# Attention and two MLPs on one core: the second MLP's weight units worked in place by a table of steps, and the first MLP's second product moved a step back

## The chip, the cores and the metric

The kernel runs on one core of a Trainium2 chip. Its time is device microseconds (us) of that core; the median of three runs of the kernel before is 884.52 us (882.35 to 887.07). The engines are named as in the profile: PE is TensorE (PEld its weight loads), DVE is VectorE, ACT is ScalarE, POOL is GpSimd, SP is SyncE, which here issues nearly all DMAs. PSUM is used as eight `banks` of 512 float32 columns.

## The reference

Attention within chunks of 64 tokens (4 x 8 heads, 576 tokens, head size 64), then two MLPs without biases over all 2304 tokens, width 512, hidden width 2048:

```python
scores = scale * np.matmul(q_c, k_c.transpose(0, 1, 2, 4, 3))
scores = scores - np.max(scores, axis=-1, keepdims=True)
attn = np.exp(scores)
attn = attn / (np.sum(attn, axis=-1, keepdims=True) + 1e-09)
out = np.matmul(attn, v_c)
...
h = x @ w_in            # first MLP
g = h - np.tanh(h)
return (g @ w_out).astype(np.float32)
...
h = x @ w_in            # second MLP
sp = np.where(h > 20.0, h, np.log1p(np.exp(np.minimum(h, 20.0))))
g = h * np.tanh(sp)
return (g @ w_out).astype(np.float32)
```

The weights arrive as float64.

## The kernel before

**Precision.** Each factor of a large product is split into a high part (a cast to float32r on ACT) and a low part (the float32 value less the high part), and a product is three matmuls (`THREE`). So every tensor that enters the large products costs a cast and a subtraction. A float64 weight is first turned into float32 in a "unit" of 128 x 1024 values: `turned` on ACT (the high word's exponent), `low` on DVE (the low word's three top bits by a shift), `joined` on DVE (both words into one).

**First MLP.** The 2304 tokens go in blocks of 512, 256, 512, 512, 512 (`BLOCKS`), the hidden width in 16 units f. A step s is one block and one f, 80 in all: `gemm1(s)` is 12 matmuls into one of two hidden banks, then h - tanh(h) by `gap_act` (ACT: z = Square, t = Tanh), `gap_mid` (DVE: g = z times h, t = h - t), `gap_poly` (ACT: m, z) and, one step later, `gap_end` (DVE: a scalar_tensor_tensor and a copy_predicated). `hi_part` casts g on ACT and `lo_part` makes its low part, on DVE for the first 32 steps and on POOL from there. `gemm2` of a step, 12 matmuls into banks 0 to 3, stands two steps behind its `gemm1` (`lag`). After a block's last step `evacuate` copies the four banks out on ACT into two or three single buffers (`e`, `et`, `ev`) and stores them to DRAM. The even weights stay in SBUF; from block 2 on the odd ones come back through a ring of three slots (`w_again`, 21 loads of 1 MB).

**Beside it.** Block 0 also turns the first MLP's weights. The 18 attention groups of 128 tokens (scores, max and exp, norm, transpose, values) run one block ahead, one per three steps. From step 35 on (`first_job`) the second MLP's 16 units run as jobs, a new one every 2.4 steps: load, `j_turned`, `j_low`, `j_float` into another buffer `jf`, `j_sums` (four slots made from sums and differences, for a seven-product scheme in the place of eight), and for the units of w_out `j_split`: cast on ACT, low parts on POOL. The results go to DRAM (`win`, `wout`).

**Second MLP.** Three passes of 768 tokens. In a pass the first phase (`group1`, four groups of 84 matmuls of 384 columns) makes g = mish, the second (`phase2`, 56 slots of 6 matmuls) multiplies by w_out, reading g through `g_split` (cast on ACT, low part on DVE, 384 columns each, three slots ahead). `x_split` and `wf_lo` part 1 make the low parts of x and of three of seven weight slots on POOL. At the end of `group1`'s last group three sums over g (`add`, `sub`, `sub`) come before phase 2's next splits on DVE.

**What sets the order.** Each engine runs its instructions in the order in which the code issues them; there is no scheduler. In a step that order is given by the lists `inner`, `cast`, `tail`, `job` (filled ahead, by step) and by the loop's body. SP's DMAs stand in one queue in the same order.

Of the kernel before, what the change touches and what calls it, by code (L numbers as in the profile page):

```python
# [13 lines left out]
I64 = mybir.dt.int64  # L14
AF = mybir.ActivationFunctionType
# [27 lines left out]
AHEAD = 4  # L43
# [3 lines left out]
def attn_moe_moe(ctx, tc, qkv, w1, w2, out):  # L47
# [12 lines left out]
    xp = es.enter_context(tc.tile_pool(name="x", bufs=2))  # L60
# [89 lines left out]
    streamed = [(b, f) for b in range(2, NB) for f in range(1, NF, 2)][RING:]  # L150
    ring = [(2, f) for f in range(1, 2 * RING, 2)] + streamed

    def w_again():

        while streamed:
            k = ring.index(streamed[0])
            b, f = ring[k - RING]
            if done <= b * NF + f:
                return
            W.pop(f)  # L160
            f = streamed.pop(0)[1]
            W.pop(f, None)
            W[f] = rp.tile([P, 2, 2 * DM], F32R, tag=f"r{k % RING}", name=f"w{f}", bufs=1)
            nc.sync.dma_start(out=W[f][:].bitcast(F32).rearrange("p c n -> p (c n)"), in_=w1s[f])


    JR, JF, SA, SB = {}, {}, {}, {}

    def j_load(n):
        JR[n] = pools["j"].tile([P, 2 * DM], I64, tag="raw", name="jraw", bufs=2)  # L170
        nc.sync.dma_start(out=JR[n], in_=w2[n])

    def j_turned(n):
        turned(JR[n])

    def j_low(n):
        low(JR[n])

    def j_float(n):
        t = JF[n] = pools["j"].tile([P, 8, 2 * P], F32, tag="jf", name="jf", bufs=2)  # L180
        joined(JR.pop(n), t[:, 1:5].rearrange("p q n -> p (q n)"))

    def j_sums(n):

        t = JF[n]
        sub(t[:, 5:7], t[:, 3:4].to_broadcast([P, 2, 2 * P]), t[:, 2:5:2])
        sub(t[:, 7], t[:, 4], t[:, 5])
        sub(t[:, 0], t[:, 1], t[:, 7])
        if n < NJ:
            JF.pop(n)  # L190
            nc.sync.dma_start(out=win[n][:, :4], in_=t[:, 4:])
            nc.sync.dma_start(out=win[n][:, 4:], in_=t[:, :3])

    def j_split(n, part):
        t = JF[n] if part == 0 else JF.pop(n)
        m, src = (4, t[:, 4:]) if part == 0 else (3, t[:, :3])
        o = (SA, SB)[part][n] = pools["j"].tile([P, 2, m, 2 * P], F32R, tag=f"s{part}", name="js", bufs=1)
        nc.scalar.copy(o[:, 0], src)
        sub(o[:, 1], src, o[:, 0].bitcast(F32), nc.gpsimd)

    def j_store(n, part):
        h, jj = divmod(n - NJ, 4)
        o = (SA, SB)[part].pop(n)
        m = (slice(0, 4), slice(4, 7))[part]
        for c in range(2):
            nc.sync.dma_start(out=wout[h][:, m, c, jj], in_=o[:, c].bitcast(F32))


    QKV, E, ET, MX, RD, BK = {}, {}, {}, {}, {}, {}
# [78 lines left out]
    def a_part(i, part):  # L288
        b = block_of[i]
        o = (i - first[b]) * P  # L290
        if (0, b) not in XL:
            XL[0, b] = xp.tile([P, 2, KD, TMAX], F32R, tag="x", name="x")
# [8 lines left out]
    steps = [(b, f) for b in range(NB) for f in range(NF)]  # L301
# [33 lines left out]
    def evacuate(b):  # L335

        t, o = BLOCKS[b], first[b] * P
        XL.pop((0, b), None)
        for m in range(KD):
            if b + 1 < NB:  # L340
                tag = ("e", "et", "ev")[m % (3 if "j" in pools else 2)]
                y = pools["j" if tag == "ev" else "a"].tile([P, TMAX], F32, tag=tag, name="ev", bufs=1)
            else:
                y = out_tile()[:].rearrange("p m n -> p (m n)")
            y = y[:, :t]
# [9 lines left out]
    def temp(s, tag, dt=F32):  # L355
        return ep.tile([P, TMAX], dt, tag=tag, name=tag)[:, :BLOCKS[steps[s][0]]]
# [11 lines left out]
    def gap_act(s):  # L368
# [16 lines left out]
    def hi_part(s):  # L385
        if max(lag(s), lag(s - 1)) > LAG and s % 2:
# [4 lines left out]
        nc.scalar.copy(o[:, 0, :BLOCKS[steps[s][0]]], GF[s])  # L391

# [11 lines left out]
    for f in range(NF - 2):  # L404
        w_load(f)
# [18 lines left out]
    def run(*todo):  # L424
# [11 lines left out]
        (a_load, lead), (a_load, lead + 1), (w_load, NF - 2), (w_load, NF - 1),  # L436
# [4 lines left out]
    inner, tail, head, mid, post = {}, {}, {}, {}, {}  # L441
# [4 lines left out]
    for b in range(1, NB):  # L446
        for q in range(BLOCKS[b] // P):
# [4 lines left out]
            at(tail, s, (a_first, i))  # L452
# [434 lines left out]
```

## Time and profile before

| | us |
|---|---|
| median of three runs | 884.52 |
| the profiled execution | 882.82 |
| its span on the core | 881.0 |
| PE busy | 816.8 (93%) |
| DVE busy | 673.2 (76%) |
| ACT busy | 501.9 (57%) |
| POOL busy | 192.6 (22%) |

The busy times are unions of instructions, so a matmul that is stretched counts as busy. The chain of work that ended last spends 47% of the span on PE and 33% on DVE. Step 0's `gemm1` starts at 24.9 us, block 2 (the first step with 512 columns after block 1) at 182, block 4 at 390; the last `gemm2` of the first MLP ends at 509.5 and the last matmul at 876.5. In the second MLP the three passes begin at 500, 635 and 758 and their second phases at 569, 693 and 816.

### The profile page before, as it was taken

What the parts mean: (1) busy time and instruction counts of PE and PEld (TensorE: products, weight loads), DVE (VectorE), ACT (ScalarE), POOL (GpSimd) and SP (SyncE); (2) the same over time, 40 slices, a digit from 0 to 9 for tenths busy, and PEclk for the clock granted to TensorE, in tenths of its full rate; (3) what the DMA queues carried; (4) which work ended last, traced back from release to release, by engine and by line L of the source; (5) the groups of instructions that cost most, each with busy time, mean ns of one, the idle gap of its engine ahead of it and who ended that gap; (6) DMA issues with size and microseconds to landing.
All of it is one profiled execution on the core that took longest, in us unless ns stands there. A gap on an engine that the chain in (4) does not pass through costs nothing.

```text
span 881.0 us, 13693 instructions
## 1 busy us (share of the span) xinstructions
PE 816.8 (93%) x5244; PEld 723.5 (82%) x5244; DVE 673.2 (76%) x952; ACT 501.9 (57%) x851; POOL 192.6 (22%) x128
## 2 busy tenths in 40 slices
PE   7899898999899989898997879989999999999997
PEld 6677688987677777676775679988999899999897
DVE  6999867866989888888964548778578787587663
ACT  4878865665566656566654544545545456445543
POOL 0001100011332332333335322123022042122000
PEclk9999999999999999999999999999999999999999
DMA  9964716636578787759582054487632787443783
GB/s 378 420 230 108 173 31 228 216 96 242 205 260 328 254 288 271 249 185 338 206 280 84 25 197 119 171 283 262 247 102 88 279 283 294 140 129 124 257 274 123
DMA packets 57777, 186.48 MB, mean 212 GB/s; under 512 B 4592, under 2 KB 32752, under 8 KB 44528
## 3 DMA queue, kind: packets, MB, share of 16 engines
q1 hardware_dynamic: 56272, 180.37, 58.2%
q0 software_dynamic: 1440, 5.24, 3.2%
q8 instruction: 41, 0.67, 0.3%
q14 instruction: 24, 0.20, 0.1%
HBM read 140.51 MB, written 39.85 MB: 205 GB/s over the span
## 4 chain that ended last, share of the span: by engine, by line
PE 47%; DVE 33%; ACT 6%; DMA 6%; issue 5%; POOL 2%; SPq 1%; ACTq 0%; DVEq 0%; POOLq 0%
PE banks L577 19%; PE banks L666 16%; PE banks L328 6%; PE banks L319 5%; DVE g L364 4%; DVE jf L81 4%; DVE jf L112 3%; DVE g L365 3%; DVE g L377 2%; DVE t L81 2%; DVE s L81 2%; DMA w<-wf 2%; DVE wf L112 1%; POOL xo L81 1%; DMA x<-ev 1%
## 5 line engine op out<-in xcount | busy, mean ns | idle before, releaser
L328 PE MATMUL banks<-go,w 128*128 128x512 f32 (+1 forms) x960 | 224.9, 382 | 15.2 <-POOL go L81 6.6
L319 PE MATMUL banks<-x,w 128*128 128x512 f32 (+1 forms) x960 | 216.4, 374 | 7.5 <-DMA w<-wf 2.7
L328 PEld LDWEIGHTS banks<-go,w 128*128 128x128 f32 x960 | 168.7, 192 | 55.6 <-POOL go L81 10.1
L319 PEld LDWEIGHTS banks<-x,w 128*128 128x128 f32 x960 | 168.3, 189 | 43.6 <-DVE w L81 3.9
L666 PE MATMUL banks<-s,w 128*128 128x384 f32 x1008 | 180.0, 339 | 11.4 <-DVE s L81 11.4
L666 PEld LDWEIGHTS banks<-s,w 128*128 128x128 f32 x1008 | 176.0, 190 | 15.0 <-DVE s L81 15.0
L577 PE MATMUL banks<-xo,w 128*128 128x384 f32 x1008 | 176.1, 334 | 4.7 <-ACT o L346 2.2
L577 PEld LDWEIGHTS banks<-xo,w 128*128 128x128 f32 x1008 | 174.9, 188 | 5.9 <-ACT o L346 2.6
L81 DVE TENSOR_TENSOR s<-g,s 128x384 fp32r<-128x384 f32 x168 | 96.6, 616 | 41.3 <-ACT s L654 41.0
L81 POOL TENSOR_TENSOR go<-g,go 128x512 fp32r<-128x512 f32 x48 | 61.9, 1290 | 264.4 <-ACT go L391 243.0
L654 ACT CAST s<-g 128x384 fp32r<-128x384 f32 x168 | 79.9, 511 | 47.6 <-PE banks L666 44.3
L391 ACT CAST go<-g 128x512 fp32r<-128x512 f32 (+1 forms) x80 | 46.2, 578 | 90.2 <-DVE g L365 90.1
L81 POOL TENSOR_TENSOR w<-wf,w 128x768 fp32r<-128x768 f32 x24 | 44.3, 1846 | 155.1 <-ACT w L550 149.2
L550 ACT CAST w<-wf 128x1024 fp32r<-128x1024 f32 (+1 forms) x48 | 44.8, 936 | 47.4 <-DMA wf<-win 31.5
L84 DVE TENSOR_TENSOR o<-o,banks 128x768 f32<-128x768 f32 x39 | 37.1, 951 | 40.5 <-ACT o L597 15.5
L377 DVE TENSOR_TENSOR g<-z,banks 128x512 f32<-128x512 f32 (+1 forms) x80 | 49.9, 624 | 21.8 <-ACT t L372 21.8
L371 ACT ACTIVATE z<-banks 128x512 f32<-128x512 f32 (+1 forms) x80 | 43.9, 548 | 34.5 <-PE banks L319 34.5
L364 DVE SCALAR_TENSOR_TENSOR g<-z,g 128x512 f32<-128x512 f32 (+1 forms) x80 | 58.8, 734 | 4.6 <-ACT z L383 4.6
L365 DVE COPY_PREDICATED g<-m,t 128x512 f32<-128x512 int16 (+1 forms) x80 | 59.2, 741 | 2.8
L589 ACT ACTIVATE g<-g 128x768 f32<-128x768 f32 x36 | 30.5, 848 | 44.4 <-DVE g L84 44.4
L81 DVE TENSOR_TENSOR t<-banks,t 128x512 f32<-128x512 f32 (+1 forms) x80 | 50.4, 630 | 0.0
L383 ACT ACTIVATE z<-z 128x512 f32<-128x512 f32 (+1 forms) x80 | 47.2, 589 | 5.2 <-DVE g L377 2.8
(60 smaller groups left out, 787.0 us busy)
## 6 DMA issues: line engine op xcount, KB each, us to landing
w<-wout SPq DMA_DIRECT2D x42, 1024.0 KB, 5.0
w<-w1s SPq DMA_DIRECT2D x21, 1024.0 KB, 6.3
w<-w SPq DMA_DIRECT2D x16, 1024.0 KB, 19.8
jraw<-w SPq DMA_DIRECT2D x16, 1024.0 KB, 6.0
qkv<-qkv SPq DMA_DIRECT2D x18, 768.0 KB, 6.8
wf<-win SPq DMA_DIRECT2D x24, 512.0 KB, 4.1
wf<-win SPq DMA_DIRECT2D x24, 384.0 KB, 3.1
w1s<-w SPq DMA_DIRECT2D x8, 1024.0 KB, 8.9
```

Of the source, the lines that this page charges most:

```text
L81: (eng or nc.vector).tensor_tensor(o, a, b, op=ALU.subtract)
L319: nc.tensor.matmul(ps, w[:, a, k * P:(k + 1) * P], x[:, c, k, :BLOCKS[b]], start=n == 0, stop=n == 3 * KD - 1)
L328: nc.tensor.matmul(banks[:, m, :t], w[:, a, DM + m * P:DM + (m + 1) * P], g[:, c, :t], start=f == 0 and n == 0, stop=f == NF - 1 and n == 2)
L364: nc.vector.scalar_tensor_tensor(g, z, PK, g, op0=ALU.add, op1=ALU.mult)
L365: nc.vector.copy_predicated(g, m.bitcast(I16), t)
L377: nc.vector.tensor_tensor(g, z, ph, op=ALU.mult)
L383: nc.scalar.activation(z, z, AF.Square, scale=SQ_SCALE, bias=SQ_BIAS)
L391: nc.scalar.copy(o[:, 0, :BLOCKS[steps[s][0]]], GF[s])
L550: nc.scalar.copy(t[:, 0], WF[p, j, part])
L577: nc.tensor.matmul(ps, w[:, x, c % 4, k * P:(k + 1) * P], XO[p][:, a, y, k], start=m == 0 and n < 4, stop=m == 5, skip_group_check=n > 3)
L654: nc.scalar.copy(t[:, 0], src)
L666: nc.tensor.matmul(ps[:, m], w[:, x, j % 4, m * P:(m + 1) * P], s[:, y], start=n == 0 and j == 0 and q < 4, stop=n == 2 and j == NJ - 1, s ...
```

## The change

- `gemm2` stands three steps behind from step 36 on, and `hi_part` and `lo_part` of a step run two steps after it instead of one; `hi_part` now stands between Square and Tanh. The transposes of attention (`a_turn`) stand behind the step's `gemm2`, before it stood ahead.
- The second MLP's units stay in one buffer of five (`unit`): `j_low` is an ACT activation, `j_join` writes in place, the sums fill the unit's other half, and the low parts are subtractions in place on DVE. A table `JOBS` gives each operation of each unit its step.
- `evacuate` copies all four banks into the block's own buffer of x, which is free by then.
- The order of f is turned round in block 3, so the ring reloads 15 units.
- q and k are loaded apart from v, and three first-MLP weights later than before.
- In the second MLP all low parts are on DVE (POOL keeps `lo_part` only); `g_split` takes 768 columns, two ahead; phase 2 has 28 slots of 12 matmuls; the sums over the last group's g move into phase 2's slots 0, 1 and 18. At its start `evacuate` stands before `wf_hi(0, 1, 1)`, and that weight's load is issued earlier.

```diff
-AHEAD = 4
+AHEAD = 2
...
-    streamed = [(b, f) for b in range(2, NB) for f in range(1, NF, 2)][RING:]
+    ring = [1, 3, 5]
+    def plan_stream():
+        at_slot, used = dict(enumerate(ring)), {k: -1 for k in range(RING)}
+        for s in range(2 * NF, NS):
+            f = steps[s][1]
+            if f % 2 == 0 or s < first_job and f >= 2 * RING:
+                continue
+            k = next((k for k in at_slot if at_slot[k] == f), None)
+            if k is None:
+                k = min(used, key=used.get)
+                streamed.append((f, k, used[k], at_slot[k]))
+                at_slot[k] = f
+            used[k] = s
...
+    def j_load(n):
+        J[n] = pools["j"].tile([P, 2 * DM], I64, tag="unit", name="unit", bufs=5)
     def j_low(n):
-        low(JR[n])
+        nc.scalar.activation(words(J[n], I32)[0], words(J[n], U32)[0], AF.Copy, scale=7.499 * 2.0 ** -32)
+    def j_join(n):
+        t = JT[n] = J[n][:].bitcast(F32).rearrange("p (q n) -> p q n", q=8)
+        joined(J[n], t[:, :4].rearrange("p q n -> p (q n)"))
+    def j_sum(n, part):
+        t = JT[n]
+        if part == 0:
+            sub(t[:, 4:6], t[:, 0:1].to_broadcast([P, 2, 2 * P]), t[:, 2:4])
+        else:
+            sub(t[:, 6], t[:, 3], t[:, 4])
+            sub(t[:, 0], t[:, 1], t[:, 6])
...
-        sub(o[:, 1], src, o[:, 0].bitcast(F32), nc.gpsimd)
+    def j_hi(n, part):
+        h = HI[n, part] = pools["j"].tile([P, 4 - part, 2 * P], F32, tag=f"hi{part}", name="jhi", bufs=1)
+        nc.scalar.copy(h[:].bitcast(F32R), JT[n][:, HALVES[part]])
+    def j_lo(n, part):
+        t = JT[n][:, HALVES[part]]
+        sub(t, t, HI[n, part])
...
-    steps = [(b, f) for b in range(NB) for f in range(NF)]
+    steps = [(b, f if b != 3 else NF - 1 - f) for b in range(NB) for f in range(NF)]
...
+            ev = xp.tile([P, 2 * KD * TMAX], F32, tag=f"x{b % 2}", name="ev")
         for m in range(KD):
-                tag = ("e", "et", "ev")[m % (3 if "j" in pools else 2)]
-                y = pools["j" if tag == "ev" else "a"].tile([P, TMAX], F32, tag=tag, name="ev", bufs=1)
+            y = ev[:, m * TMAX:m * TMAX + t]
             nc.scalar.copy(y, banks[:, m, :t])
...
         nc.scalar.activation(z, ph, AF.Square)
+        run(*between)
         nc.scalar.activation(t, ph, AF.Tanh)
...
-        return LAG + (short(s) or s > 0 and short(s - 1))
+        return LAG + (short(s) or s > 0 and short(s - 1) or s > first_job)
...
-    JOBS = [12 * n // 5 for n in range(12)] + [28, 30, 32, 34]
+    JOBS = [
+        (8, 35, 38, 38, 39, 39, 39, 40, 41, 40, 42),
+        (0, 35, 38, 39, 40, 42, 42),
...
+    DONE = [(j_turn, cast), (j_low, cast), (j_join, job), (j_sum, job, 0), (j_sum, job, 1),
+            (j_hi, cast, 0), (j_lo, job, 0), (j_hi, cast, 1), (j_lo, job, 1)]
...
-            sub(lo, src, hi.bitcast(F32), nc.gpsimd)
+            sub(lo, src, hi.bitcast(F32))
...
-        sub(t[:, 1], WF.pop((p, j, part)), t[:, 0].bitcast(F32), nc.gpsimd if part else nc.vector)
+        sub(t[:, 1], WF.pop((p, j, part)), t[:, 0].bitcast(F32))
...
+        at(extra, 0, (g_sum, p, NK - 1, 0))
+        at(extra, 1, (g_sum, p, NK - 1, 1))
+        at(extra, 18, (g_sum, p, NK - 1, 2))
...
+        behind = s - 1 if s <= late else s - 2
+        if s > late:
+            gap_act(s, [(hi_part, behind)] if behind >= late else [])
+            if behind >= late:
+                lo_part(behind)
+            gap_mid(s)
+            run(*inner.pop(s, []))
+            second(s)
+            run(*outer.pop(s, []))
+            gap_poly(s)
```

Here `second(s)` issues the `gemm2`s that are due, and `outer` holds the `a_turn`s.

DVE in block 2, the last operations of one unit before the change (`jraw`, `jf` are the unit's buffers, `g`, `z`, `t`, `m` those of h - tanh(h), `rd` and `e` attention's):

```order
L112 SCALAR_TENSOR_TENSOR jf<-jraw 128x1024
L364 SCALAR_TENSOR_TENSOR g<-z,g 128x512
L365 COPY_PREDICATED g<-m,t 128x512
L377 TENSOR_TENSOR g<-z,banks 128x512
L81 TENSOR_TENSOR t<-banks,t 128x512
L257 TENSOR_REDUCE rd<-e 128x8
L258 TENSOR_SCALAR rd<-rd 128x8
L259 RECIPROCAL rd<-rd 128x8
L260 TENSOR_TENSOR e<-e,rd 128x512
L81 TENSOR_TENSOR jf<-jf 128x512
L81 TENSOR_TENSOR jf<-jf 128x256 x2
```

The same engine there with the change (`jhi` is a unit's high part):

```order
L82 TENSOR_TENSOR unit<-unit,jhi 128x1024
L390 SCALAR_TENSOR_TENSOR g<-z,g 128x512
L391 COPY_PREDICATED g<-m,t 128x512
L404 TENSOR_TENSOR g<-z,banks 128x512
L82 TENSOR_TENSOR t<-banks,t 128x512
L82 TENSOR_TENSOR unit<-unit,jhi 128x768
L82 TENSOR_TENSOR unit<-unit 128x512
L82 TENSOR_TENSOR unit<-unit 128x256 x2
```

The units' low parts (1024 and 768 columns) now stand on DVE, and the table puts two units' work side by side.

ACT in block 2 before (`js` is the high part of a w_out unit, `et` attention's transposed tile):

```order
L371 ACTIVATE z<-banks 128x512
L372 ACTIVATE t<-banks 128x512
L391 CAST go<-g 128x512
L382 ACTIVATE m<-z 128x512
L383 ACTIVATE z<-z 128x512
L198 CAST js<-jf 128x1024
L103 ACTIVATE jraw<-jraw 128x1024
L272 COPY et<-banks 128x512
```

ACT there with the change:

```order
L397 ACTIVATE z<-banks 128x512
L418 CAST go<-g 128x512
L399 ACTIVATE t<-banks 128x512
L409 ACTIVATE m<-z 128x512
L410 ACTIVATE z<-z 128x512
L104 ACTIVATE unit<-unit 128x1024
L189 ACTIVATE unit<-unit 128x1024
```

The cast of g has moved ahead of Tanh and belongs to a step further back; L189 is the shift that was on DVE.

DVE at the end of the last pass's first phase before (`g_6299` is the last group's g, `s` the split parts, `o` the sums):

```order
L81 TENSOR_TENSOR s<-g_5943,s 128x384 x2
L81 TENSOR_TENSOR s<-g_6063,s 128x384
L84 TENSOR_TENSOR g_6299<-o,banks 128x768 x2
L84 TENSOR_TENSOR g_6299<-g_6299 128x768
L81 TENSOR_TENSOR g_6299<-g_6299 128x1536
L81 TENSOR_TENSOR g_6299<-g_6299 128x768
L81 TENSOR_TENSOR s<-g_6063,s 128x384
```

The same place with the change:

```order
L82 TENSOR_TENSOR s<-g_6830,s 128x768
L82 TENSOR_TENSOR s<-g_6950,s 128x768
L85 TENSOR_TENSOR g_7186<-o,banks 128x768 x2
L82 TENSOR_TENSOR s<-g_7070,s 128x768
L85 TENSOR_TENSOR g_7186<-g_7186 128x768
L82 TENSOR_TENSOR s<-g_7186,s 128x768
L82 TENSOR_TENSOR g_7186<-g_7186 128x1536
L82 TENSOR_TENSOR s<-g_6830,s 128x768
```

The splits that phase 2 needs first are no longer behind the three sums.

## Rows read from the trace of the kernel before

**Rows 1.** Busy time by stretch: us, length, each engine's, PEclk, DMA share, GB/s.

```profile
182.00:390.00 208.00, 194.27 (x1325) 155.45 (x1324) 172.67 (x242) 125.14 (x213) 63.55 (x41) 0.99 0.67 239
390.00:509.00 119.00, 106.27 (x432) 81.94 (x431) 83.05 (x110) 65.50 (x108) 47.34 (x31) 0.97 0.56 192
509.00:881.00 372.00, 351.40 (x1995) 346.47 (x1993) 264.78 (x333) 184.45 (x300) 72.25 (x40) 0.99 0.59 199
```

**Rows 2.** PE's matmuls in order of time, a stretch of block 2 without waits.

```profile
278.64 2.97 PE L319 MATMUL banks<-x,w 128*128 128x512 f32 x12
...
289.72 2.97 PE L319 MATMUL banks<-x,w 128*128 128x512 f32 x12
```

**Rows 3.** The chain that ended last (start, us, what): a first phase without waits.

```profile
635.30 58.26 PE banks L577 x336
```

**Rows 4.** Whom PE waited for, 182 to 390: us, times, longest.

```profile
PE banks L267 <- DVE e L260: 7.5, 5, 2.1
PE banks L284 <- ACT et L272: 5.7, 5, 2.6
```

**Rows 5.** The same, 390 to 509.5.

```profile
PE banks L328 <- POOL go L81: 6.6, 8, 0.9
```

**Rows 6.** The same, 509 to 881.

```profile
PE banks L666 <- DVE s L81: 11.4, 11, 1.9
```

**Rows 7.** POOL and DVE in order of time, a low part of a unit.

```profile
436.75 2.49 POOL L81 TENSOR_TENSOR js<-jf,js 128x1024 fp32r<-128x1024 f32 x1 [0.85 <-ACT js L198]
...
436.91 2.88 DVE L364 SCALAR_TENSOR_TENSOR g<-z,g 128x512 f32<-128x512 f32 x1
```

**Rows 8.** Groups of instructions, 182 to 509: busy us, mean ns, idle before.

```profile
L81 POOL TENSOR_TENSOR go<-g,go 128x512 fp32r<-128x512 f32 x48 | 61.9, 1290 | 264.4 <-ACT go L391 243.0 <-DMA w<-w1s 14.2 <-issue 7.1
...
L364 DVE SCALAR_TENSOR_TENSOR g<-z,g 128x512 f32<-128x512 f32 x48 | 41.0, 855 | 2.0 <-ACT z L383 2.0
...
L377 DVE TENSOR_TENSOR g<-z,banks 128x512 f32<-128x512 f32 x48 | 32.4, 676 | 10.8 <-ACT t L372 10.8
L112 DVE SCALAR_TENSOR_TENSOR jf<-jraw 128x1024 int32<-128x1024 int32 x16 | 32.0, 2002 | 0.0
...
L81 DVE TENSOR_TENSOR jf<-jf 128x512 f32<-128x512 f32 x16 | 18.8, 1173 | 0.0
...
L103 ACT ACTIVATE jraw<-jraw 128x1024 f32<-128x1024 f32 x16 | 18.1, 1132 | 4.5 <-DMA jraw<-w 4.5
...
L108 DVE TENSOR_SCALAR jraw<-jraw 128x1024 int32<-128x1024 int32 x16 | 12.7, 796 | 3.0 <-DMA jraw<-w 3.0
```

**Rows 9.** The same view, 40 to 110, where POOL computes nothing.

```profile
L112 DVE SCALAR_TENSOR_TENSOR wf<-w 128x1024 int32<-128x1024 int32 x12 | 14.6, 1219 | 3.0 <-DMA w<-wf 2.9
...
L364 DVE SCALAR_TENSOR_TENSOR g<-z,g 128x512 f32<-128x512 f32 x10 | 6.8, 683 | 0.0
...
L81 DVE TENSOR_TENSOR w<-wf,w 128x1024 fp32r<-128x1024 f32 x3 | 3.6, 1200 | 0.0
```

**Rows 10.** Whom DVE waited for, 182 to 509.

```profile
DVE x L81 <- ACT x L296: 15.0, 8, 2.3
```

**Rows 11.** Whom PE waited for, 25 to 182.

```profile
PE banks L267 <- DVE e L260: 2.6, 1, 2.6
```

**Rows 12.** The chain in order of time, at the second MLP's start.

```profile
506.72 3.06 DMA wf<-win
```

**Rows 13.** Groups of instructions over the whole span, second MLP.

```profile
L81 DVE TENSOR_TENSOR g<-g 128x1536 f32<-128x1536 f32 x12 | 21.1, 1758 | 0.4
...
L81 DVE TENSOR_TENSOR g<-g 128x768 f32<-128x768 f32 x12 | 11.5, 959 | 1.3
...
L81 DVE TENSOR_TENSOR xt<-xs 128x192 f32<-128x192 f32 x12 | 4.2, 348 | 0.0
```

**Rows 14.** The same view, 820 to 881, a second phase.

```profile
L81 DVE TENSOR_TENSOR s<-g,s 128x384 fp32r<-128x384 f32 x53 | 27.9, 556 | 16.5 <-ACT s L654 16.5
```

**Rows 15.** DMA issues of the page: count, KB each, us to landing.

```profile
w<-w1s SPq DMA_DIRECT2D x21, 1024.0 KB, 6.3
```

More of the change, by code (lines that the diff above doesn't have):

```diff
@@ L146, in w_keep @@
         nc.sync.dma_start(out=w1s[f], in_=W[f][:].bitcast(F32).rearrange("p c n -> p (c n)"))
-    streamed = [(b, f) for b in range(2, NB) for f in range(1, NF, 2)][RING:]
-    ring = [(2, f) for f in range(1, 2 * RING, 2)] + streamed
-    def w_again():
[L155 to L161, printed above, removed]
+    ring = [1, 3, 5]
+    last_use = {}
@@ L391, in hi_part, with spare @@
         nc.scalar.copy(o[:, 0, :BLOCKS[steps[s][0]]], GF[s])
+    XG = {}
+    def spare(k, n):
+        if not XG:
+            XG[0] = xp.tile([P, KD, 2 * TMAX], F32, tag="x1", name="spare")
+        return XG[0][:, k, :n]
     def lo_part(s):
@@ L403, in attn_moe_moe @@
         a_load(i)
-    for f in range(NF - 2):
+    for f in range(NF - 3):
         w_load(f)
@@ new lines, in attn_moe_moe @@
+    DONE = [(j_turn, cast), (j_low, cast), (j_join, job), (j_sum, job, 0), (j_sum, job, 1),
+            (j_hi, cast, 0), (j_lo, job, 0), (j_hi, cast, 1), (j_lo, job, 1)]
+    ends = 0
+    for n, start, *when in JOBS:
+        if start > first_job:
+            at(job, start, (j_load, n))
+        for (what, plan, *part), s in zip(DONE, when):
+            at(plan, s, (what, n, *part))
+            if what == j_lo:
+                at(job, s + 1, (j_store, n, *part))
+        if n < NJ:
+            at(job, when[-1] + 1, (j_store, n, 0), (j_store, n, 1))
+        at(job, max(when) + 1, (j_done, n))
+        ends = max(ends, max(when) + 1)
@@ L612, in group1 @@
             mish(g[:, 1], g[:, 1])
-            for k in range(AHEAD - 1):
+            for k in range(AHEAD):
                 g_split(p, k)
@@ L711, in phase2 @@
[L711 to L727 removed]
+            n = 4 * (p + 1)
@@ L728, in phase2, with second @@
                 ended2(p, q)
             run(*extra.pop(k, []))
+    late = first_job + 1
+    XFROM = 4 * NF + 5
+    def second(s):
+        nonlocal done
+        while done < min(NS, s + 1) and done + lag(done) <= s:
+            gemm2(done)
+            done += 1
     for s in range(NS):
@@ L779, in attn_moe_moe @@
             wf_hi(0, 0, 0)
-        run(*inner.get(s, []))
-        for u in units(s, 2) if not later else []:
-            w_float(u)
-        while done < min(NS, s + 1) and done + lag(done) <= s:
-            gemm2(done)
-            done += 1
-        for u in units(s, 3):
-            w_turned(u)
-            w_low(u)
-        run(*tail.get(s, []))
+        run(*tail.pop(s, []))
         w_again()
         run(*job.pop(s, []))
+        if s == XFROM:
+            for c in range(4):
+                x_load(c)
         if s == ends:
@@ L794, in attn_moe_moe @@
             pools["x"] = ctx.enter_context(tc.tile_pool(name="late", bufs=1, side="right"))
[L795 to L796 removed]
             wf_load(0, 1, 0)
[L798 to L806 removed]
+        c = s - ends - 3
+        if 0 <= c < 4:
+            x_split(c, 0, 1)
+            x_split(c, 1, 1)
+        if 0 <= c + 2 < 4:
+            x_sum(c + 2, 0)
+            x_sum(c + 2, 1)
+        if s == ends + 4:
+            t = WF[0, 0, 0] = spare(0, 8 * P).rearrange("p (m n) -> p m n", m=4)
+            nc.sync.dma_start(out=t, in_=win[0][:, :4])
         if s == NS - 3:
             wf_lo(0, 1, 0)
[L809 removed]
+    assert not streamed and not job and not cast and not tail and not inner and not outer and ends + 6 < NS
     nc.scalar.preload_act_table_set("mish")
+    gap_end(NS - 1)
     wf_lo(0, 0, 0)
[L813 removed]
+    hi_part(NS - 2)
+    lo_part(NS - 2)
+    gemm2(NS - 3)
     hi_part(NS - 1)
     lo_part(NS - 1)
+    wf_load(0, 1, 1)
     for n in range(2):
         both(0, 0, n)
[L818 removed]
+    for s in range(NS - 2, NS):
         gemm2(s)
+    assert done == NS - 3
     XL.clear()
+    XG.clear()
     W.clear()
```

356 lines of the change are left out of this document (182 added, 174 removed).

## The prediction

> **What bounds the kernel now.** I read the busy times by stretch first, then PE's own pace, then whom PE waited for in each stretch, and last what made those engines late. I call 182 to 390 B (blocks 2 and 3), 390 to 509 C (block 4 and the end of the first MLP), 509 to 881 D (the second MLP), and what lies before A.
>
> PE's pace where nothing holds it: two steps, that is 48 matmuls of 512 columns, take 289.72 - 278.64 = 11.08, so a step takes 5.54 [rows 2]; 336 matmuls of 384 columns take 58.26, so one takes 0.1734 [rows 3]. C holds 16 first and 18 second products, 17 steps' worth, and 24 narrow matmuls: 94.2 + 4.2 = 98.4 of its 119 us, so about 20 are lost. D holds 2016 - 24 = 1992 narrow matmuls, 345.4, and 4.5 from the last matmul to the end: of 372 about 22 are lost. In B PE is idle 208 - 194.3 = 13.7, and the clock of 0.99 adds some 2: 15.7 lost [rows 1]. So B, C and D lose 58 us together, and PE sets the rest.
>
> Why it is lost: in B PE waits for attention's norm on DVE (7.5) and its transposed tile on ACT (5.7) [rows 4]; in C for the low part of g on POOL (6.6) [rows 5]; in D for the splits on DVE (11.4) [rows 6]. Behind the first two stands DVE, which is made late by POOL: beside a low part of a unit that POOL computes from 436.75 for 2.49, a DVE instruction that starts at 436.91 takes 2.88 and ends just behind it [rows 7]; where POOL computes nothing the same instruction takes 0.683 [rows 9]. Three groups show the sum: L364 41.0 instead of 48 x 0.683, L112 32.0 instead of 16 x 1.219, the 512-column difference 18.8 instead of 16 x 0.683 [rows 8, 9]: 8.2 + 12.5 + 7.9 = 28.6 us of DVE lost in B and C, against 63.6 + 47.3 = 110.9 of POOL work [rows 1], about a quarter of it.
>
> The Trainium skill says it as a rule (SBUF — State Buffer, "Who interferes with whom"): a DVE instruction with two SBUF inputs and a GpSimd instruction that reads SBUF exclude each other for the whole instruction, and one with at most one SBUF input does not contend. By that rule the trace agrees, with the 2.88.
>
> **The change part by part.** *Units and DVE in B and C.* DVE is busy 172.7 + 83.1 = 255.7 there [rows 1]. Away goes the shift, 12.7 [rows 8]. Away go the 28.6 lost to POOL, at first in full. On it come the low parts of eight w_out units, 8 x (1.200 + 0.959) = 17.3 [rows 9, 13], and those of x, 4 x (0.75 + 0.96) = 6.8 (576 columns lie between the 0.683 of 512 and the 0.959 of 768). That makes 238.5. POOL keeps 48 low parts of g, 61.9 [rows 8]; how much of them DVE waits out is not shown, since the order is new: nothing at best, 61.9 at worst. Now the cast of g stands between Square and Tanh, so POOL's work falls beside `gap_mid`, whose two operations read PSUM and show no stretch (L377 takes 0.676 beside all of POOL's work [rows 8], as its undisturbed fellow L364). As long as DVE is on time the price is nothing; when it is late by two operations, it meets them. I take a quarter as before, 16. DVE also waits for ACT's cast of x, 15.0 over eight groups [rows 10]; that stays, since the unit's casts still stand ahead of it on ACT (in four of the table's steps two of them, about 2). Together 238.5 + 16 + 15 = 269.5, against a PE that needs 327 - 35.7 = 291. So DVE fits, with 7% to spare, and not in every step: the table puts up to 6.4 us of DVE work on a step of 5.54.
>
> *The shift on ACT.* 16 activations. The nearest row is the other activation over the same strided words, 1.13 [rows 8]; integers in and out could cost twice that at worst, and nothing less than 1.05 is seen for 1024 columns. I take 1.13: 18 us more on ACT, whose 125.1 + 65.5 [rows 1] become 209 of 291; 227 at worst. It is hidden while ACT has a quarter free.
>
> *One more step for g.* Cast, low part and second product now have a step (5.54) between `gap_end` and the cast, so a late DVE no longer holds up PE by that way; the waits of [rows 5] go. The price is that Tanh, and DVE's h - t behind it, start 0.62 later in each step; that is free where DVE is late by as much, and 48 x 0.62 = 30 of DVE idle at worst. `a_turn` behind the second product gives the norm 2.8 more, which covers its longest wait of 2.1 [rows 4]. The transposed tile is not helped: ACT still has the unit's casts ahead of that copy.
>
> *B:* of 15.7 I leave 10 (eight attention groups at 1.2), gain 6, with 0 to 13 as ends. *C:* no attention, POOL freed of units and x; I leave 4 of 20, gain 16, ends 9 and 18.
>
> *D.* All of POOL's work goes to DVE: per pass 8 weight parts of 0.96 and four pairs of x parts, about 14.5. The splits become 28 x 0.96 = 26.9 for 56 x 0.556 = 31 [rows 13, 14]. A group of the first phase then asks DVE for 5 x 0.96 + 0.96 + 1.76 + 0.96 + 2 x 1.2 + 2 x 0.96 = 12.8 of its 14.57; a second phase for 26.9 + 5 x 0.96 + 3.7 (the sums over g) + 16 x 0.348 = 5.6 (the sums over x) + 6.8 (their low parts) + 3.4 (weights) = 51 of 58.3 [rows 9, 13, 14]. Both fit, and nothing on POOL stretches them any more. The wait at the second phase's start (longest 1.9 [rows 6]) goes because the sums of the last group, 0.96 + 1.76 + 0.96, no longer stand ahead of the splits. A slot is 2.08, a split is ready some 1.9 after its buffer is free and is needed 4.16 after. At D's start evacuation waited behind a weight whose load took 3.06 [rows 12]; that load is now issued earlier, but the next one (0, 0, 1) stands behind the evacuation's stores, so I leave 2.5 there, and 1 per pass: 5.5 of 22, gain 16.5, ends 10 and 19.
>
> *A.* When block 0 is evacuated, the third copy waits for a store to free its buffer, ACT and DVE come to attention's norm late, and PE waits 2.6 for it [rows 11]. Now all copies have room: gain 2.6, and 0.4 for the smaller first load; ends 0 and 5. The weights' turning in block 0 is as before.
>
> Sum: 3 + 6 + 16 + 16.5 = 41.5. The span falls from 881.0 to 839.5; with the 1.8 that the profiled execution had around its span, 841.3. That execution took 882.8, 1.7 under the median of the runs shown, which spread by 4.7. I say 841.
>
> **Rivals.** *POOL's lock stays.* If DVE waits out every remaining low part, it needs 238.5 + 61.9 + 15 = 315 in B and C, against PE's 291; with what PE loses beside that, B and C gain about 5 instead of 22. For it: once DVE is late by two operations each step meets POOL again, and the delay keeps itself up. Against: DVE has slack in most steps. 881 - 3 - 5 - 16.5 + 1.8 = 858, from 850 to 866.
>
> *All is hidden.* B keeps 3, C 2, D 3, A gains 4: 12.7 + 18 + 19 + 4 = 53.7, so 829 (824 to 832). For it: the table keeps DVE under PE nearly everywhere. Against: the order on ACT that made 15.0 in [rows 10] is unchanged.
>
> *Slower: the ring.* With the product three steps behind, a ring slot is free two steps (11.1) before its next use, where it was three (16.6). A reload took 6.3 [rows 15]. From 11.1 on each further us is a wait of PE at each of 15 reloads. It decides against the change at 46/15 = 3.1 beyond, so at 14.2 for a landing, more than twice the row: 888 and up. For it: five unit loads of 1 MB stand ahead of the first reload, and B already moves 239 GB/s with the DMA engines 67% busy [rows 1]; against it six reloads fewer.
>
> *Nothing comes of it:* DVE becomes the bound of D too, as its 12.8 of 14.57 slip: 880 to 889.
>
> **How the numbers follow.** Forecast 0.58 (832 to 850), lock 0.17, all hidden 0.15, slower 0.06, nothing 0.04. A measurement tells about 0.5%, 4.4 us, from no change. The likeliest gives 841; the range goes from 824 to 862, and leaves out the last two cases and the end of the second. Faster 0.90, same 0.04, slower 0.06.
>
> **What would show it.** Right: in B and C no DVE group with its mean far over that of [rows 9]; PE's waits for POOL's g gone; in the second MLP both phases at 58.3 to 59, without waits for splits; PE's remaining waits in B at attention's values, for ACT. Wrong: L364's counterpart still over 0.8 (the lock), first products that wait for a DMA of w (the ring), a unit shift on ACT well over 1.2, or second phases over 61.

## The result, and the profile after

The changed kernel takes 857.44 us (median, 855.59 to 859.85) against 885.25 for the kernel before in the same session: ratio 0.969, 95% interval 0.9653 to 0.9727. It is 27.8 us faster; the prediction was 841 (824 to 862), its likeliest case 832 to 850. Its profiled execution has a span of 855.2 at a clock of 0.985.

Cut by the starts of `gemm1` of steps 32 and 64, by the end of the last `gemm2` and by the end of the span, the two traces compare so (us; the stretches that the prediction calls A to D):

| | before | after | gained | forecast |
|---|---|---|---|---|
| A, to the start of block 2 | 181.9 | 179.9 | 2.0 | 3 |
| B, blocks 2 and 3 | 208.1 | 212.0 | -3.9 | 6 |
| C, block 4 | 119.5 | 106.5 | 13.0 | 16 |
| D, second MLP | 371.6 | 356.8 | 14.7 | 16.5 |

Of the 15.6 that the span missed, 9.9 are in B. (With the product three steps behind, B holds one second product fewer and C one more, 32 and 19 for 33 and 18, 2.8 us each way. The forecast did not count this. Counted alike, B loses 6.7 and C gains 15.8, so nearly the whole miss is in B.)

The busy times of the same three stretches, for [rows 1] (length, then PE, PEld, DVE, ACT and POOL busy, PE's clock, DMA share, GB/s):

```profile
180.00:392.00 212.00, 196.06 (x1314) 156.87 (x1313) 166.14 (x242) 136.18 (x228) 41.73 (x30) 0.97 0.62 222
392.00:498.00 106.00, 103.25 (x444) 83.85 (x444) 84.70 (x118) 67.73 (x113) 24.47 (x18) 0.98 0.54 185
498.00:855.00 357.00, 349.71 (x1994) 348.50 (x1992) 258.61 (x289) 172.93 (x214) 0.00 (x0) 1.00 0.60 204
```

DVE is no busier than before in B and C together (250.8 for 255.7) and POOL's work is down to 66 there, yet PE's clock in B fell from 0.99 to 0.97. Whom PE waited for in B, for [rows 4] (two waits of 0.7 are left out, so 15.9 in all):

```profile
PE banks L311 <- ACT et L299: 10.0, 5, 3.7
PE banks L346 <- DMA w<-w1s: 3.1, 1, 3.1
PE banks L355 <- POOL go L82: 1.4, 2, 0.8
```

The norm's 7.5 are down to 0.7, but the transposed tile costs 10.0 instead of 5.7, and the first ring reload costs 3.1. In C, for [rows 5]:

```profile
PE banks L355 <- POOL go L82: 1.9, 2, 1.0
PE banks L355 <- ACT go L418: 0.8, 1, 0.8
```

In D, for [rows 6]; no wait for a split is left:

```profile
PE banks L631 <- ACT w L606: 2.6, 1, 2.6
PE banks L631 <- DVE w L82: 0.4, 1, 0.4
```

Some groups of instructions between 180 and 498, for [rows 8] (busy us, mean ns, idle before and its releaser):

```profile
L82 POOL TENSOR_TENSOR go<-g,go 128x512 fp32r<-128x512 f32 x48 | 66.2, 1380 | 311.0 <-ACT go L418 290.9 <-DVE g L390 9.5 <-DVE unit L82 6.5
L391 DVE COPY_PREDICATED g<-m,t 128x512 f32<-128x512 int16 x48 | 48.4, 1009 | 1.7
L390 DVE SCALAR_TENSOR_TENSOR g<-z,g 128x512 f32<-128x512 f32 x48 | 40.5, 844 | 1.1 <-ACT z L410 1.1
L404 DVE TENSOR_TENSOR g<-z,banks 128x512 f32<-128x512 f32 x48 | 32.5, 678 | 31.9 <-ACT t L399 31.8
L410 ACT ACTIVATE z<-z 128x512 f32<-128x512 f32 x48 | 30.3, 632 | 61.2 <-DVE g L404 61.0
L113 DVE SCALAR_TENSOR_TENSOR unit<-unit 128x1024 int32<-128x1024 int32 x16 | 20.6, 1285 | 0.0
L189 ACT ACTIVATE unit<-unit 128x1024 int32<-128x1024 uint32 x16 | 18.2, 1138 | 0.0
L82 DVE TENSOR_TENSOR unit<-unit 128x512 f32<-128x512 f32 x16 | 15.1, 941 | 0.2
```

The units' join (L113) is almost undisturbed now, 1285 ns for 2002 before. But both operations of `gap_end` are stretched (L390 844, L391 1009), and ACT stands 61 us in wait of DVE's g before its second Square (L410). The means hide how: 7 of the 48 L390 took 1.76 to 1.79 us and 12 of the 48 L391 1.70 to 1.88, in 19 different steps, and the rest were undisturbed. One such meeting, in order of time (other rows are left out):

```profile
375.32 1.40 POOL L82 TENSOR_TENSOR go<-g,go 128x512 fp32r<-128x512 f32 x1 [3.51 <-ACT go L418]
375.60 1.72 DVE L391 COPY_PREDICATED g<-m,t 128x512 f32<-128x512 int16 x1
377.22 0.66 DVE L404 TENSOR_TENSOR g<-z,banks 128x512 f32<-128x512 f32 x1
377.98 0.63 ACT L410 ACTIVATE z<-z 128x512 f32<-128x512 f32 x1 [1.72 <-DVE g L404]
378.51 1.12 ACT L104 ACTIVATE unit<-unit 128x1024 f32<-128x1024 f32 x1
379.53 1.18 ACT L189 ACTIVATE unit<-unit 128x1024 int32<-128x1024 uint32 x1
380.56 0.62 ACT L299 COPY et<-banks 128x512 f32<-128x512 f32 x1
381.23 0.69 PE L311 MATMUL banks<-et,v 64*64 64x64 f32 x32 [3.28 <-ACT et L299]
381.85 4.59 PE L355 MATMUL banks<-go,w 128*128 128x512 f32 x12
```

It is read from top to bottom: the low part of g starts 0.28 before DVE's copy_predicated, which therefore ends 1.0 late; the multiplication behind it, and ACT's second Square behind that, are late by as much; a unit's two activations stand between that Square and the copy of the transposed tile; and PE waits 3.28 for it. The wait costs more than its length: from 382.24 on the granted clock stands at its lower level (1.2 for 2.4 GHz), and twelve matmuls take 4.59 that take 2.97 in [rows 2]. The low part was released by ACT's cast (L418), not by DVE: that proved to be the point.

### The profile page after: what moved, and what is told of

Its sections match the earlier page's. It is cut to its first block, busy times and chain, and to the rows that moved or that the text cites. A ratio compares the mean times of both kernels' runs of the same rounds, so it can differ in the third digit from the quotient of the medians.

```text
span 855.2 us, 13350 instructions
## 1 busy us (share of the span) xinstructions
PE 816.2 (95%) x5244; PEld 730.6 (85%) x5244; DVE 662.3 (77%) x916; ACT 503.6 (59%) x783; POOL 75.7 (9%) x64
## 4 chain that ended last, share of the span: by engine, by line
PE 57%; DVE 24%; DMA 7%; ACT 6%; issue 5%; SPq 1%; POOL 0%; DVEq 0%; ACTq 0%; POOLq 0%
PE banks L732 21%; PE banks L631 20%; PE banks L355 8%; PE banks L346 7%; DVE unit L82 3%; DVE g L390 3%; DVE g L404 3%; DMA w<-w1s 3%; DVE t L82 2%; DMA w<-wf 2%; DVE unit L113 2%; DVE wf L113 1%; DMA wout<-unit 1%; DVE g L391 1%; ACT unit L104 1%
## 5 line engine op out<-in xcount | busy, mean ns | idle before, releaser
L346 PE MATMUL banks<-x,w 128*128 128x512 f32 (+1 forms) x960 | 218.7, 376 | 8.6 <-DMA w<-w1s 3.1
L355 PEld LDWEIGHTS banks<-go,w 128*128 128x128 f32 x960 | 172.4, 194 | 44.8 <-POOL go L82 4.7
L732 PEld LDWEIGHTS banks<-s,w 128*128 128x128 f32 x1008 | 178.1, 188 | 0.0
L82 DVE TENSOR_TENSOR s<-g,s 128x768 fp32r<-128x768 f32 x84 | 79.9, 957 | 44.8 <-ACT s L719 44.4
L719 ACT CAST s<-g 128x768 fp32r<-128x768 f32 x84 | 69.6, 835 | 62.4 <-PE banks L732 57.2
L82 POOL TENSOR_TENSOR go<-g,go 128x512 fp32r<-128x512 f32 x48 | 66.2, 1380 | 311.0 <-ACT go L418 290.9
L410 ACT ACTIVATE z<-z 128x512 f32<-128x512 f32 (+1 forms) x80 | 47.2, 589 | 63.9 <-DVE g L404 62.9
L404 DVE TENSOR_TENSOR g<-z,banks 128x512 f32<-128x512 f32 (+1 forms) x80 | 50.1, 626 | 41.1 <-ACT t L399 41.0
L82 DVE TENSOR_TENSOR w<-wf,w 128x1024 fp32r<-128x1024 f32 (+1 forms) x53 | 58.2, 1099 | 24.1 <-ACT w L606 23.6
L391 DVE COPY_PREDICATED g<-m,t 128x512 f32<-128x512 int16 (+1 forms) x80 | 67.8, 847 | 2.8
L606 ACT CAST w<-wf 128x768 fp32r<-128x768 f32 (+1 forms) x47 | 43.8, 934 | 39.2 <-DMA wf<-win 24.9
L390 DVE SCALAR_TENSOR_TENSOR g<-z,g 128x512 f32<-128x512 f32 (+1 forms) x80 | 58.2, 728 | 3.7 <-ACT z L410 3.7
L418 ACT CAST go<-g 128x512 fp32r<-128x512 f32 (+1 forms) x80 | 45.8, 573 | 7.6 <-DVE g L391 7.5
```

Of the source, the lines that this page charges most:

```text
L82: (eng or nc.vector).tensor_tensor(o, a, b, op=ALU.subtract)
L346: nc.tensor.matmul(ps, w[:, a, k * P:(k + 1) * P], x[:, c, k, :BLOCKS[b]], start=n == 0, stop=n == 3 * KD - 1)
L390: nc.vector.scalar_tensor_tensor(g, z, PK, g, op0=ALU.add, op1=ALU.mult)
L391: nc.vector.copy_predicated(g, m.bitcast(I16), t)
L404: nc.vector.tensor_tensor(g, z, ph, op=ALU.mult)
L410: nc.scalar.activation(z, z, AF.Square, scale=SQ_SCALE, bias=SQ_BIAS)
```

## The experiments

All ratios are to the kernel before, with 95% intervals; the changed kernel's is 0.969 [0.9653, 0.9727]. Two theories stood at first: (1) the changed order of attention on ACT and PE costs the time in B; (2) POOL's low part, with the cast two steps behind, now stretches `gap_end`. A third came up on the way, as theory 2 of the run with the transposes back in front: the later cast costs by itself, since it makes Tanh late.

**The waits taken away one at a time.**

```diff
-            at(tail, s + 2, (a_turned, i))
+            at(early if s + 2 > first_job + 1 else tail, s + 2, (a_turned, i))
...
             gap_poly(s)
+            run(*early.pop(s, []))
```

> The changed kernel, with attention's copy of the transposed tile (a_turned) issued on ACT ahead of the step's unit activations and casts, from step 37 on. Theory 1 (ACT's order): PE's waits for that copy, 10.0 us in blocks 2 and 3, come from the unit's two activations (1.13 each) that stand ahead of it; they fall under 2.5, the half-clock stretches behind them go, and the time falls from 857.4 to 843 to 849. Rival (DVE's lateness): the copy is late because the Square of the step waits for a late DVE; then at least 6 of the 10.0 stay and the time is 853 to 857. Second rival: the waits go, but what was hidden behind them (second products that wait for g) takes their place: 855 to 857.

Measured: 852.47, ratio 0.9642 [0.9627, 0.9656], between the two ranges. The waits for `et` fell only from 10.0 to 8.1, and L410 waited 68.8 for DVE, more than the 61 before. ACT's order has a part in it, but ACT is late ahead of the copy.

```diff
-        (9, 35, 41, 41, 44, 44, 45, 46, 47, 46, 47),
-        (1, 35, 42, 43, 45, 45, 46),
-        (10, 35, 43, 44, 46, 48, 48, 49, 50, 49, 51),
+        (9, 38, 41, 41, 44, 44, 45, 46, 47, 46, 47),
+        (1, 39, 42, 43, 45, 45, 46),
+        (10, 40, 43, 44, 46, 48, 48, 49, 50, 49, 51),
```

> The changed kernel, with only two unit loads at step 35 and the next three at steps 38, 39 and 40 instead of all five at step 35. If the first ring reload (15.9 us to landing, where a slot leaves 11.1) is late because the five loads of 1 MB stand ahead of it, it lands in 6 to 9, PE's wait of 3.1 for it and the half-clock stretch behind it go, and the time falls by 3 to 5, to 852 to 854. Rival: the units' jobs are the bound there and the wait only moves to the next wait for the transposed tile: 856 to 858.

Measured: 856.56, ratio 0.9688 [0.9674, 0.9703]. The wait for w1s went, so the unit loads ahead of it were its cause. But PE now waited 13.2 for `et` instead of 10.0: the gain went to the next wait, since attention was late anyway.

```diff
-            at(outer if s + 2 > first_job + 1 else inner, s + 2, (a_turn, i))
+            at(inner, s + 2, (a_turn, i))
```

> The changed kernel with attention's transposes (a_turn) back ahead of the step's second product on PE; cast and second product stay a step later. Theory 1 (the transposes' place): behind the second product the transposed tile is 2.8 us later, and PE's wait for its copy is what blocks 2 and 3 lose; back in front, these waits (10.0) fall under 2, and the time is 844 to 850. Theory 2 (the cast between Square and Tanh, which makes Tanh and so DVE late): the waits stay above 6, the time is 854 to 858.

Measured: 854.88, ratio 0.9669 [0.9643, 0.9696]; L390 and L391 stay at 845 and 1052. Whom PE waited for in B:

```profile
PE banks L294 <- DVE e L287: 10.4, 5, 3.4
PE banks L346 <- DMA w<-w1s: 3.2, 1, 3.2
PE banks L311 <- ACT et L299: 2.2, 2, 1.1
```

The same 12 or so come back as waits for the norm. Where the transposes stand only decides which wait is the visible one; against theory 1.

**POOL's low part itself.**

```diff
-        sub(GO[s][:, 1, :t], ..., nc.gpsimd if s >= 2 * NF else nc.vector)
+        sub(GO[s][:, 1, :t], ...)               # always DVE
```

> The changed kernel, with the low part of g on DVE in all steps, so that POOL computes nothing. DVE gets 48 x 0.68 = 33 us more and loses the 25 us by which four of its groups are stretched beside POOL. If the stretch (the lock) is what costs in blocks 2 and 3, the groups run undisturbed, PE's waits there fall by half or more and the time is 845 to 855. If DVE's load and the order on ACT cost, it is slower: 860 to 875, with PE waiting for DVE.

Measured: 850.94, ratio 0.9629 [0.9597, 0.9662]. With POOL idle L390 and L391 take 686 and 751 ns, so the whole stretch was POOL's doing. DVE gets 48 more subtractions, and the kernel is still 6.5 faster. PE's waits in B did not fall by half: the waits for `et` remain at 8.9 of 12.1. DVE has that work now, which would explain them but was not tried apart. This shows the lock (DVE and POOL holding each other up), but is no clean cure.

```diff
-    late = first_job + 1
+    late = NS        # cast and low part one step behind, behind gap_end and gap_mid
-        return LAG + (short(s) or ... or s > first_job)
+        return LAG + (short(s) or ...)          # product two behind
```

(Here `a_turn` stands ahead of the second product again.)

> The changed kernel without the step more for g: cast and low part one step behind, second product two, the transposes ahead of the second product, as before the change; the units in place, their table, the evacuation and the second MLP as changed. If the step more gave block 4 its 13 us, PE's waits for POOL's low part and ACT's cast of g come back there: block 4 longer by 8 to 13, time 866 to 872. Rival: POOL freed of the units gave it, and the step more gives little: 855 to 861.

Measured: 844.65, ratio 0.9552 [0.9538, 0.9566], below both ranges; L390 684, L391 749, and ACT waits elsewhere:

```profile
L410 ACT ACTIVATE z<-z 128x512 f32<-128x512 f32 x48 | 30.4, 633 | 1.5
L418 ACT CAST go<-g 128x512 fp32r<-128x512 f32 x48 | 29.9, 622 | 39.6 <-DVE g L391 39.2
```

Without the part of the change that was to keep a late DVE from holding up PE, the kernel is 12.8 us faster. In this order the cast waits for `gap_end` of the step, so POOL starts behind DVE, however late DVE is.

```diff
+            run(*outer.pop(s, []))              # the same, a_turn behind the second product
```

> The kernel of the run without the step more for g (844.65), with only the transposes moved behind the second product again. Theory 1 (the transposes' place): the waits for the copy come back, 8 to 12 us, and the time is 853 to 858. Theory 2 (the cast's place): it stays at 843 to 847.

Measured: 845.67, ratio 0.9562 [0.9539, 0.9585], the same within what can be told. The cast's step makes the difference, and the transposes' place none.

**The two explanations of that pulled apart.** The kernel with the early cast differs in three things: what POOL waits for, where Tanh stands on ACT, and the product's distance. So everything was left as the change has it, and POOL alone was made to wait for DVE:

```diff
             if behind >= late:
+                if behind >= 2 * NF:
+                    g = GF[s - 1][:, :8]
+                    sub(ep.tile([P, 8], F32, tag="tie", name="tie", bufs=1), g, g, nc.gpsimd)
                 lo_part(behind)
```

> The changed kernel with one small extra POOL instruction (a subtraction over 128 x 8 of the newest g) ahead of each low part of g, so that the low part starts only when DVE has finished the gap_end of the step, as it did before the change. The cast, Tanh, the transposes, the product three steps behind and the ring window stay as the change has them. Theory (POOL's low part meets gap_end because the cast now goes by PE's pace and no longer by DVE's): L390's counterpart falls from 0.844 to 0.69 to 0.73 and L391's from 1.009 to 0.75 to 0.80, 15 to 20 us of DVE over the 48 steps, ACT's wait for its second Square falls from 61 to under 25, and the waits for the transposed tile shrink: blocks 2 and 3 from 212 to 203 to 208, total 846 to 853. Rival (the later cast costs by itself: Tanh stands 0.62 later on ACT, and the product three behind): the two stretched groups stay as they are or fall without moving the end, total 856 to 858. Third possibility: the low part ends too late for its product, PE waits for go at every step, total over 860.

Measured: 839.71, ratio 0.95 [0.9475, 0.9525], better than the theory's 846 to 853: one instruction of 0.2 us more per step makes the kernel 17.7 us faster. ACT's wait fell to 34.4, not under 25. The groups of DVE, ACT and POOL:

```profile
L391 DVE COPY_PREDICATED g<-m,t 128x512 f32<-128x512 int16 x48 | 36.0, 751 | 1.7
L390 DVE SCALAR_TENSOR_TENSOR g<-z,g 128x512 f32<-128x512 f32 x48 | 33.0, 687 | 1.1 <-ACT z L410 1.1
...
L410 ACT ACTIVATE z<-z 128x512 f32<-128x512 f32 x48 | 30.4, 633 | 34.4 <-DVE g L404 34.2
...
L82 POOL TENSOR_TENSOR go<-g,go 128x512 fp32r<-128x512 f32 x48 | 62.3, 1298 | 99.2 <-ACT go L418 98.8 <-issue 0.2 <-ACT m L409 0.2
L82 POOL TENSOR_TENSOR tie<-g 128x8 f32<-128x8 f32 x42 | 8.5, 202 | 189.6 <-DVE g L391 180.7 <-PE banks L355 8.9
```

The same attention group as above, in order of time (blocks 2 and 3 now end 16 us earlier; other rows are left out):

```profile
362.10 0.75 DVE L391 COPY_PREDICATED g<-m,t 128x512 f32<-128x512 int16 x1
362.73 0.68 DVE L404 TENSOR_TENSOR g<-z,banks 128x512 f32<-128x512 f32 x1
362.99 0.20 POOL L82 TENSOR_TENSOR tie<-g 128x8 f32<-128x8 f32 x1 [4.20 <-DVE g L391]
363.15 1.30 POOL L82 TENSOR_TENSOR go<-g,go 128x512 fp32r<-128x512 f32 x1
363.50 0.63 ACT L410 ACTIVATE z<-z 128x512 f32<-128x512 f32 x1 [0.75 <-DVE g L404]
363.92 1.35 DVE L82 TENSOR_TENSOR unit<-unit,jhi 128x768 f32<-128x768 f32 x1
```

The low part now runs beside L404, which reads PSUM and keeps its 0.68. PE's waits for `et` in B fall to 1.7, B takes 196.1 instead of 212.0, C 104.8, and D is unchanged at 356.8. PE's waits in B fall by 10.3, from 15.9 to 5.6. The granted clock stands at its lower level for 13.6 us of B without the tie and for 3.4 with it, and 10.2 less at half speed are worth 5.1: together 15.4 of the 15.9 that B gains. Tanh's place and the product's distance are as in the change, so it is the meeting that costs, and not these. The Trainium skill has the matching rule (SBUF — State Buffer, "Who interferes with whom"): issue order decides which of the two engines waits. By that rule the traces agree: the POOL operation that starts 0.28 ahead costs DVE 1.0, and one that starts behind `gap_end` costs `gap_end` nothing (the end of it still meets a unit's low part, the last row: 1.35 for 0.95). The prediction's sentence on that section leaves out the exception that the section makes for DVE's two-port modes.

**The second MLP.** The kernel before with the low parts of x and of the weights on DVE:

```diff
-            sub(lo, src, hi.bitcast(F32), nc.gpsimd)
+            sub(lo, src, hi.bitcast(F32))
-        sub(t[:, 1], ..., nc.gpsimd if part else nc.vector)
+        sub(t[:, 1], ...)
```

> The kernel before with one edit: the low parts of x and of the weights' part 1 for the second MLP on DVE instead of POOL. If the lock between POOL and DVE costs the second MLP most of its loss, its 371.6 us become 361 to 365, the waits of the second phases fall from 11.4 to about 5.5 (three starts of 1.9), and the time falls by 7 to 11, to 873 to 877. Rival: DVE has no room for 43 us more and the second MLP stays or grows: 883 to 892.

Measured: 870.59, ratio 0.9841 [0.9808, 0.9873], more than expected, since block 4, where the first pass's x is split, gains too (113.4 for 119.5). D takes 365.2 instead of 371.6, and the waits for splits halve:

```profile
PE banks L666 <- DVE s L81: 5.6, 3, 1.9
```

The reverse in the changed kernel, with those low parts (of x only from the second pass on) on POOL:

> The changed kernel with the second MLP's low parts of x (from the second pass on) and of the weights' part 1 back on POOL. If the lock costs there, sums and splits are stretched again and the second MLP grows from 356.8 by 4 to 9, the time is 861 to 866. Rival: the wider splits, two ahead, cover the stretch: 856 to 859.

Measured: 858.62, ratio 0.9706 [0.9681, 0.9731], intervals that overlap; D alone grows by 2.4. All of that lies in the first pass's first phase (60.0 for 57.6), where PE waits once, 1.3, for a weight on POOL; the first run above, whose second MLP is the change's own, took 58.9 there. Every later phase is as long as in the changed kernel. With wide splits and the sums moved, POOL's work there hardly matters.

The three sums over the last group's g put back ahead of the splits:

```diff
-        if jj < NJ // 2 - 1:
-            for k in range(3):
-                g_sum(p, jj, k)
+        for k in range(3):
+            g_sum(p, jj, k)
```

> The changed kernel with the three sums over the last group's g put back where they were, ahead of the second phase's splits, in each of the three passes; the splits stay wide and on DVE. The prediction's step: the sums (0.96 + 1.76 + 0.96 on DVE) ahead of the splits are what PE waited for at the second phases' starts, 1.9 at most. Then PE waits again for s at the start of each second phase, 1.5 to 3 a pass: the second MLP goes from 356.8 to 361 to 366, total 861 to 866. Rival (with POOL off DVE's way the splits are ready anyway, and the gain came from the lock and the wide splits): 856 to 859, no wait for s over 0.5.

Measured: 858.75, ratio 0.9717 [0.9688, 0.9746]; the totals can't be told apart, and PE's waits are back, one in each pass:

```profile
PE banks L731 <- DVE s L82: 3.7, 3, 1.2
```

Yet a second phase takes only 0.46 more, 59.82 for 59.36, since PE runs faster behind the wait (below). D takes 359.7 for 356.8, but the other half of that lies in the first pass's first phase again. So of D's gain of 14.7, taking the low parts off POOL is worth about 6.4 in the old order of work, and the sums' place 1.4 in the new one. The rest was not run apart: wide splits, the second MLP's start, and what these do together.

**Faster versions.** The kernel with the early cast, and the weight (0, 0, 1) loaded ahead of the evacuation's stores:

```diff
     wf_load(0, 2, 0)
+    wf_load(0, 0, 1)                    # and no longer issued where it was
     evacuate(NB - 1)
```

> The kernel with the cast one step behind (which ran at 844.65), and the weight (0, 0, 1) of the second MLP loaded ahead of the evacuation's stores in place of behind them. Prediction's step: 2.5 at the second MLP's start are the wait for that weight. Expected: the wait of the first phase's first matmuls for w on ACT (1.8 there, 2.6 in the changed kernel) and on DVE (1.0) falls by 2 to 3: 841 to 843. Rival: the DMA engines are shared with the evacuation's stores and x's loads, so the load only takes longer, or the next tensor is late by as much: 844 to 846.

Measured: 840.0, ratio 0.9494 [0.9469, 0.952]; PE's waits for w at the second MLP's start fall from 6.0 (4.6 for ACT, 1.4 for DVE) to 2.8. (What is left are the 1.8 and 1.0 that the expectation names; the 2.8 and 0.4 behind them went.) Last, the changed kernel with the tie, this load and the later unit loads:

> The changed kernel with the tied low part (which ran at 839.71), with the weight (0, 0, 1) loaded ahead of the evacuation's stores (which gave 4.7 in the kernel with the early cast), and with the three unit loads 9, 1 and 10 issued three to five steps later, so that the first ring reload does not stand behind them (there the wait for w1s, 3.1 to 3.3, went, and the gain with it, since attention was late). Theory (with the stretch gone DVE and ACT have room, so a wait that is taken away is not replaced): 839.7 - 3.3 - 2.5 to 4.7 = 831.7 to 834. Rival (the gains move to the next wait again, as with the loads before): 836 to 840.

Measured: 833.32 (832.98 to 834.61), ratio 0.9433 [0.9407, 0.946], within the theory's 831.7 to 834. All that PE waits for between 180 and 370 is

```profile
PE banks L311 <- ACT et L299: 4.4, 5, 2.2
PE banks L355 <- POOL go L82: 0.6, 1, 0.6
```

and its clock is 1.00. The wait of 3.3 for w1s went and most of it came back elsewhere (`et` 4.4 for 1.7); B is shorter all the same, 193.7 for 196.1, with a clock of 1.00 for 0.99. D gives 3.6.

## Why the prediction was right in the whole and wrong in B

**The whole** is right by the range and not by the argument. 857.44 misses the likeliest case (832 to 850); it lies in the range because that takes in most of the lock rival, which came instead. Two of the prediction's own signs of being wrong were seen: L364's counterpart over 0.8 (0.844), and a first product that waits for a DMA of w (once, 3.1).

**The step that failed** is "Units and DVE in B and C", with its sentence that POOL's work falls beside `gap_mid` and that "as long as DVE is on time the price is nothing". That read the order of one step and took it for what holds DVE and POOL together. It does not: the cast two steps behind hangs on Square, so on PE's pace, and POOL's start moves with it, while `gap_end` moves with DVE. Where DVE is late by so much that one of the two operations of `gap_end` starts behind the low part, in 19 of 48 steps, they meet. The old order had the tie by accident: cast and low part waited for `gap_end`.

The size put in for it was too small: 16 us forecast, and measured over the undisturbed 0.687, 0.751 and 0.683 it is 48 x 0.157 = 7.5 for L390, 48 x 0.258 = 12.4 for L391, 4.1 for the 512-column sums and 1.1 for the join, 25. That alone did not make DVE too slow: it is busy 250.8 in B and C, for the 238.5 + 16 = 254.5 of the sum. What failed with it is that these 16 were set against DVE's slack over the whole stretch. They fall in the steps where DVE is already late, and go on to ACT's second Square (61 us of wait, 34 with the tie), the copy of the transposed tile and PE.

**One more step for g** was right in direction, but only with POOL kept behind DVE: with the tie it is worth 844.65 - 839.71 = 4.9 over the early cast (6.0 with the transposes in the same place, 845.67); without, it costs 11.8 to 12.8. One reason shows in the traces: behind the early cast POOL starts later and still meets the units' operations. Their sums of 512 columns and low parts of 768 and 1024, which take 0.687, 0.954 and 1.222 with POOL idle, take 0.959, 1.342 and 1.541 there (845.67), and 0.784, 1.096 and 1.307 with the tie. How much of the 4.9 this is was not run apart. Its price was bounded rightly: DVE's wait for Tanh rose from 10.8 to 31.8, by 21 of the 30 put at worst. `a_turn` behind the product did what was said of it: the norm's wait went, and came back as 10.4 with the transposes in front. The transposed tile was indeed not helped.

**B**, forecast to gain 6, lost 3.9; with the tie it gains 12.0 (in both, 2.8 is the second product that moved to C). **The lock rival** named this mechanism ("once DVE is late by two operations each step meets POOL again") and 858, at a chance of 0.17. Its total was hit, though it put B and C together at 5 and they gained 9.1.

**C** gained 13.0 of 16, and 15.8 when the product that moved in is left out. Little of it came from the later cast: with the early cast C takes 104.7, with the later one 106.5, or 103.7 without that product. The low parts of x and of weights, taken off POOL in the kernel before, gave 6.1; that the units' low parts gave the rest is likely, but was not run. **The shift on ACT** took 1.138 for the 1.13 forecast.

**D** gained 14.7 of 16.5. First phases take 58.24, and the waits for splits went, as predicted. Second phases do not reach 58.3; the chain of waits shows (start, us):

```profile
615.47 58.24 PE banks L631 x336
673.72 59.36 PE banks L732 x336
```

With no wait in them a matmul takes 0.1767, not 0.1734, and the three phases lose 3.4 so: every second one takes 179 to 180 ns, the others 174. It is not the phase as such. With the sums put back, PE goes through the first of these phases, behind its wait, at 0.1742:

```profile
560.93 54.19 PE banks L731 x311
```

So the slow pace came with the phases that start without a wait, and took back most of what the wait's going gave. Why was not tried. At D's start the 2.5 left for weight (0, 0, 1) were 2.6; in the last version, with that load ahead, PE waits for no weight there.

**A** gained 2.0 of 3. **The ring rival** was half right: the wait of 3.1 came, once, behind unit loads as it said, and at no other reload.

## What to carry to other kernels

When work is given to POOL beside DVE, ask what its start waits for: if that is another engine's pace, it will meet DVE's two-input operations as soon as DVE is late, and make it later. A dependence on the DVE instruction that it must not meet, here by a POOL instruction of 0.2 us, kept it beside PSUM reads here. Look past a group's mean: 1009 ns was 36 undisturbed instructions and 12 of more than twice their time. A slack summed over a long stretch does not pay for a delay that comes in the very steps that are late already.

## What was not expected of the hardware

A copy_predicated pays for POOL like the two-input operations: 751 ns alone, 1.70 to 1.88 us in the 12 meetings. And 336 matmuls of 384 columns took 59.36 in the second phase against 58.24 in the first, both at full clock and without a wait, while behind a wait the second phase too ran at 0.1742 a matmul; the cause stays open.
